# Five of nine pairs of groups of ph in seven half-products instead of eight, with sums of x and a list schedule in the source

## The chip, the cores and the metric

The kernel runs on one core of one Trainium2 chip. The metric is the device time of one execution in microseconds (us).

## What is computed

Attention with 2 x 12 heads of 448 rows and 64 columns, then two feed-forward stages on 896 rows of 768:

```
scores = 1/8 * q @ k.T, causal;  attn = softmax(scores) @ v
x = attn, heads side by side                              # 896 x 768
h = max(max(x @ w1, x @ w2), x @ w3)                      # 768 x 768 each
y = h @ w_out                                             # 768 x 768
out = elu(y @ w_in) @ w_out2                              # 768 x 2048, 2048 x 768
```

## The kernel before

Everything after attention is kept transposed: `x[b][k]` is tile k (128 of the 768 columns of x) of batch b, 128 x 2 x 448. Plane 0 holds the high part of the numbers (float32r) and plane 1 what is left of them. A weight tile is split in the same way into hi and lo. `products` (line 213) makes one product out of three matmuls per tile (a pass is one matmul of 448 columns): hi by plane 0 (L218), hi by plane 1 (L219), lo by plane 0 (L221).

ph is the product of x with w1, w2 and w3. For each of six column blocks f and each of the three weights n there is one *group*: six tiles, three passes, two batches, 36 passes, into two PSUM banks. `keep_best` (L230) copies the first product (ScalarE, L232) and takes the maximum with the others (VectorE, L234) into `best`. After n = 2, `best` is split into h (ScalarE L537, VectorE L146).

A weight arrives in 64-bit words that hold doubles. `load_w` (L185) issues its transfer on SP (L154) and turns it into hi and lo: three integer steps on VectorE (L199, L201, L202), a lift on ScalarE (L203), a combining step on VectorE (L204), hi on ScalarE (L208), lo on VectorE (L209). The first three weights (f = 0) are converted by another chain (`ahead_steps`, L157) during attention, and b = 0 of these groups is multiplied there, in TensorE's holes.

During attention `Plan` sets the order of work on all engines: each task has costs per engine, a due time (`LEADS`) and slots, and a list scheduler picks the next. After attention the source's own order and the framework set it: f = 0 for b = 1, then f = 1 to 5, then py (h by w_out), pg and po.

GpSimd has work in attention alone: it normalises the probabilities `pr` (L346).

Of the kernel before, what the change touches and what calls it, by code (L numbers as in the profile page):

```python
# [8 lines left out]
F32 = mybir.dt.float32  # L9
# [11 lines left out]
NPAIR = H // 2  # L21
# [17 lines left out]
SBANKS = 4  # L39

# [7 lines left out]
    "values3": -1.05, "warm": 2.09, "x_hi": 1.23, "x_lo": -1.04,  # L48
# [3 lines left out]
class Plan:  # L52
# [8 lines left out]
    LAG = {"PE": 210, "ACT": 150, "DVE": 125, "POOL": 90, "DMA": 2000}  # L61
# [8 lines left out]
    def add(self, fn, args, engines, pair, after=(), takes=(), gives=(), mode=None):  # L70
        lead = LEADS.get(f"{fn.__name__}{args[0]}" if args else None, LEADS.get(fn.__name__))
# [22 lines left out]
    def order(self):  # L94
        free = dict.fromkeys(self.LAG, 0)
# [28 lines left out]
def fused_kernel(ctx: ExitStack, tc: tile.TileContext, qk, v, w1, w2, w3, wo, wi2, wo2, outT):  # L124
# [32 lines left out]
    def ahead_steps(src, n, name, pool):  # L157
# [20 lines left out]
        hi, lo = (pool.tile([128, n, 128], F32R, tag=f"a_{m}", name=f"{m}_{name}") for m in ("hi", "lo"))  # L178
# [6 lines left out]
    def load_w(src, n, name):  # L185

# [39 lines left out]
    with ExitStack() as s1:  # L226
# [10 lines left out]
        ap_w = s1.enter_context(tc.tile_pool(name="ap_w", bufs=len(AHEAD)))  # L237
        ahead, bests, last = {}, {}, {}

        with ExitStack() as s2:  # L240
# [258 lines left out]
            kept = None  # L499
            for k in range(len(AHEAD)):  # L500
                block(k, weights(k))
            with tc.manual_schedule():
# [3 lines left out]
        hp = s1.enter_context(tc.tile_pool(name="hp", bufs=2 * NK))  # L506

        ctx.enter_context(tc.tile_pool(name="pad", bufs=1, side="right")).tile([128, 24], F32, name="pad")
        yp = ctx.enter_context(tc.tile_pool(name="yp", bufs=2 * NK, side="right"))
# [10 lines left out]
        h = [[None] * NK for _ in range(B)]  # L520
        for f in range(NK):
            best = [bests.get((f, b)) or bp.tile([128, S], F32, tag=f"best{b}", name=f"best{b}_{f}") for b in range(B)]
            for n, w in enumerate((w1, w2, w3)):
                over = range(1, B) if (f, n) in AHEAD else range(B)
                if (f, n) in AHEAD:
                    hi, lo = ahead[f, n]
# [99 lines left out]
```

## Time and profile before

| | |
|---|---|
| median of three runs | 505.23 us (504.86 to 505.77) |
| the profiled execution's own time | 505.17 us |
| its span, first to last instruction | 503.4 us |
| TensorE busy (matmul) | 497.0 us, 99% |
| VectorE busy | 313.9 us, 62% |
| ScalarE busy | 233.4 us, 46% |
| GpSimd busy | 41.0 us, 8% |
| granted TensorE clock | 1.00 |

A matmul of 448 columns is shown with 368 ns, but they are pipelined; what counts is how far apart they start. Durations on VectorE and ScalarE also overlap slightly with the next instruction's.

### The profile page before, as it was taken

The page shows a single profiled execution, that of the slowest core. Times are in us where ns is not written, and L with a number is a line of the kernel's source. Part 1 is how long each engine was busy: PE and PEld are TensorE (multiplying, and loading weights), DVE is VectorE, ACT ScalarE, POOL GpSimd, SP SyncE. Part 2 cuts the span into 40 slices and gives each one's busy share as a digit, 9 for nine tenths or more (in the row PEclk, how much of TensorE's full clock was granted, in tenths as well). Part 3 has the DMA queues.
Part 4 walks back from the last instruction along what each step waited for, and adds up shares of the span by engine and source line. Part 5 has one row for each costly group of instructions (what it writes and reads, how often), then busy time and mean ns, then how long its engine had stood idle before and what let it go on. Part 6 is the DMA issues. An engine that isn't in the chain of part 4 may idle for free.

```text
span 503.4 us, 6946 instructions
## 1 busy us (share of the span) xinstructions
PE 497.0 (99%) x2600; PEld 424.8 (84%) x2600; DVE 313.9 (62%) x664; ACT 233.4 (46%) x481; POOL 41.0 (8%) x96
## 2 busy tenths in 40 slices
PE   8999999999999999999999999999999999999997
PEld 3555757899999999999999999999999999999996
DVE  4999995477756656565656766776776544555310
ACT  5998794443333233332334665665664222222100
POOL 3475361000000000000000000000000000000000
PEclk9999999999999999999999999999999999999999
DMA  6626510055332331332332332332233434344000
GB/s 204 230 84 210 202 57 22 0 188 189 126 101 88 126 123 67 126 105 84 125 125 64 125 124 68 124 125 74 94 116 89 131 127 147 87 146 141 1 36 36
DMA packets 13969, 55.88 MB, mean 111 GB/s; under 512 B 1520, under 2 KB 3568, under 8 KB 13936
## 3 DMA queue, kind: packets, MB, share of 16 engines
q1 hardware_dynamic: 13936, 55.45, 32.9%
q8 instruction: 20, 0.33, 0.3%
q14 instruction: 13, 0.11, 0.1%
HBM read 52.69 MB, written 2.75 MB: 110 GB/s over the span
## 4 chain that ended last, share of the span: by engine, by line
PE 94%; DVE 2%; DMA 1%; POOL 1%; SPq 0%; ACT 0%; issue 0%; DVEq 0%; ACTq 0%
PE ph L218 9%; PE ph L221 9%; PE ph L219 9%; PE pg L221 8%; PE po L218 8%; PE po L219 8%; PE po L221 8%; PE pg L219 8%; PE pg L218 8%; PE pt L356 4%; PE o L379 4%; PE s L309 3%; PE py L221 3%; PE py L219 3%; PE py L218 3%; DVE pr L323 1%
## 5 line engine op out<-in xcount | busy, mean ns | idle before, releaser
L218 PE MATMUL ph<-x,hi_w 128*128 128x448 f32 x216 | 79.9, 370 | 0.0
L219 PE MATMUL ph<-x,hi_w 128*128 128x448 f32 x216 | 79.5, 368 | 0.0
L219 PE MATMUL po<-g,hi_wo 128*128 128x448 f32 x192 | 70.7, 368 | 0.0
L218 PE MATMUL po<-g,hi_wo 128*128 128x448 f32 x192 | 70.7, 368 | 0.0
L219 PE MATMUL pg<-y,hi_wi 128*128 128x448 f32 x192 | 70.5, 367 | 0.0
L218 PE MATMUL pg<-y,hi_wi 128*128 128x448 f32 x192 | 70.5, 367 | 0.0
L221 PE MATMUL ph<-x,lo_w 128*128 128x448 f32 x216 | 65.0, 368 | 0.0
L221 PE MATMUL po<-g,lo_wo 128*128 128x448 f32 x192 | 56.0, 368 | 0.0
L221 PE MATMUL pg<-y,lo_wi 128*128 128x448 f32 x192 | 55.1, 367 | 0.0
L203 ACT ACTIVATE f_wo<-f_wo,lift 128x768 uint32<-128x768 int16 (+1 forms) x24 | 21.2, 884 | 53.1 <-DVE f_wo L202 53.1
L208 ACT ACTIVATE hi_wo<-f_wo 128x768 fp32r<-128x768 f32 (+1 forms) x24 | 19.0, 792 | 56.1 <-PE po L219 38.8
L221 PEld LDWEIGHTS ph<-x,lo_w 128*128 128x128 f32 x216 | 40.5, 188 | 4.1
L209 DVE SCALAR_TENSOR_TENSOR lo_wo<-f_wo,hi_wo 128x768 fp32r<-128x768 f32 (+1 forms) x24 | 21.4, 891 | 36.3 <-ACT hi_wo L208 36.3
L218 PEld LDWEIGHTS ph<-x,hi_w 128*128 128x128 f32 x216 | 40.5, 188 | 4.0
L219 PEld LDWEIGHTS ph<-x,hi_w 128*128 128x128 f32 x216 | 40.6, 188 | 4.0
L218 PEld LDWEIGHTS po<-g,hi_wo 128*128 128x128 f32 x192 | 36.0, 188 | 3.7
L219 PEld LDWEIGHTS pg<-y,hi_wi 128*128 128x128 f32 x192 | 35.9, 187 | 3.8
L221 PEld LDWEIGHTS pg<-y,lo_wi 128*128 128x128 f32 x192 | 35.9, 187 | 3.8
L221 PEld LDWEIGHTS po<-g,lo_wo 128*128 128x128 f32 x192 | 36.0, 188 | 3.6
L219 PEld LDWEIGHTS po<-g,hi_wo 128*128 128x128 f32 x192 | 36.0, 188 | 3.6
L218 PEld LDWEIGHTS pg<-y,hi_wi 128*128 128x128 f32 x192 | 35.9, 187 | 3.7
L333 ACT ACTIVATE pr<-pr,nmx 128x384 f32<-128x384 f32 (+1 forms) x72 | 35.9, 501 | 5.8 <-DVE nmx L323 5.8
(88 smaller groups left out, 789.7 us busy)
## 6 DMA issues: line engine op xcount, KB each, us to landing
raw_w<-in_w SPq DMA_DIRECT2D x18, 768.0 KB, 4.5
raw_wi<-in_wi SPq DMA_DIRECT2D x16, 768.0 KB, 4.4
raw_wo<-in_wo SPq DMA_DIRECT2D x12, 768.0 KB, 4.3
raw_wo<-in_wo SPq DMA_DIRECT2D x12, 640.0 KB, 4.0
qk<-in_qk SPq DMA_DIRECT2D x11, 448.0 KB, 5.3
v<-in_v SPq DMA_DIRECT2D x12, 256.0 KB, 3.7
out_t<-ot SPq DMA_DIRECT2D x12, 224.0 KB, 3.0
qk<-in_qk SPq DMA_DIRECT2D x1, 256.0 KB, 3.4
```

The costliest lines, as they stand in the source:

```text
L203: nc.scalar.activation(f.bitcast(U32), y, AF.Relu, bias=lift, scale=2.0 ** 19)
L208: nc.scalar.mul(hi, fb, -1.0)
L209: nc.vector.scalar_tensor_tensor(out=lo, in0=fb, scalar=-1.0, in1=hi.bitcast(F32), op0=ALU.mult, op1=ALU.subtract)
L218: nc.tensor.matmul(ps, hi[:, c, :], xs[cc][:, 0, :], start=(cc == 0), stop=False)
L219: nc.tensor.matmul(ps, hi[:, c, :], xs[cc][:, 1, :], start=False, stop=False)
L221: nc.tensor.matmul(ps, lo[:, c, :], xs[cc][:, 0, :], start=False, stop=(cc == total - 1))
L309: nc.tensor.matmul(out, us[e]["qk"][own, 0, C * i:w], us[e]["qk"][own, 1, :w], start=True, stop=True, skip_group_check=True)
L323: nc.vector.tensor_tensor_reduce(out=pr, in0=u["s", g][j or 0][:, at:at + w], in1=mask_r if i == NB else mask[:, FULL - w:], scale=-0.125, ...
L333: nc.scalar.activation(pr, pr, AF.Exp, bias=u["nmx"][:, n:n + 1], scale=-1.0, accum_out=u["l"][:, n:n + 1])
L356: nc.tensor.transpose(pt[:e - C * c, at:at + C], u["pr", j if j is None else j ^ odd, i][:, C * c:e], ident)
L379: nc.tensor.matmul(u["o"][D * j:D * (j + 1), C * c:], u["v"][:, j, c], u["th_r"][:, j ^ odd] if c == NB else u["th"][:, c, j ^ odd, C * c: ...
```

## The change

With F1 and F2 two column blocks of one weight, u and d the upper and lower three tiles of the 768 rows, and x0, x1 the batches, the four outputs x0 F1, x0 F2, x1 F1, x1 F2 take eight half-products of 9 passes (three tiles, three passes). A *unit* takes seven, in Winograd's form of Strassen's algorithm. The sums of x are made once:

```
t0 = x1u + x1d     t1 = t0 - x0u     t2 = x0u - x1u     t3 = x0d - t1
```

and for each unit four differences of weights, "13": F2u - F1u and F2d - F2u, "24": F2d - 13u and F1d - 24u. The products, in TensorE's order (a, b, d, e are PSUM banks; `seed` copies the bank a to another, on which a later product adds):

```
a  = x0u F1u          b seeded from a
s5 = t0 13u           copied out of PSUM
a += t1 24u           d seeded from a
b += x0d F1d                               -> x0 F1
a += t2 13d           e seeded from a;  a + s5 -> x1 F2
d += t3 F2d                     d + s5         -> x0 F2
e += x1d 24d                               -> x1 F1
```

There are five units: blocks 1 and 2 for w2, w3; blocks 3 and 4 for w1, w2, w3. Blocks 0, 5 and w1 of 1 and 2 are left as groups. The new order is f = 0 (b = 1), f = 5, w1 of f = 1 and 2, then the units. The sums t (tiles t0_c to t3_c, c = 0 to 2, 24 operations; 19 are placed on GpSimd and 5 on VectorE) come from both planes of x; they are then split into planes (`whole`: 12 high halves on ScalarE, 12 low halves on VectorE). The stretch from f = 0 to the first two weights of py is list-scheduled by a second `Plan`. The order within attention stays, except that the transfers of the weights for f = 5 stand behind the last v transfers and that VectorE's first step on them lies at the end of attention.

```
+HALF = NK // 2
+UNITS = ((1, 2), (3, 4))
+FIRST = NK - 1
...
+            def add_totals(plan, c, engs, at, after, lead=None):
+                t1, t2, t3, t4 = (totals[q, c] for q in range(4))
...
+                for out, a, b, op in (
+                        (t4, h21, l21, ALU.add), (t1, t4, h22, ALU.add), (t1, t1, l22, ALU.add), (t2, h11, l11, ALU.add),
+                        (t3, t2, t4, ALU.subtract), (t2, t1, t2, ALU.subtract), (t4, h12, t2, ALU.subtract),
+                        (t4, t4, l12, ALU.add)):
...
+                        engines[eng].tensor_tensor(out=out, in0=a, in1=b, op=op)
...
+            add_totals(plan, 0, {"POOL": 950}, NPAIR + HALF, [xs_done[NPAIR + HALF]], 20)
+
+            begun = {k: load_steps((w1, w2, w3)[k][FIRST], NK, f"w{k}_{FIRST}") for k in range(2)}
...
+        late_plan = Plan({"raw": 0, "f": 2, "w": 0, "u": 7, "t": 4, "s5": 2, "m": 8, "best0": 1, "best1": 2})
+        PASS = 203.0
...
+        LOAD = (("DMA", 2000), ("DVE", 560), ("DVE", 356), ("DVE", 555), ("ACT", 937), ("DVE", 958))
+        LAST = (("ACT", 848), ("DVE", 958))
...
+        def leave(n, f, b, ps, after, gives, at, more=None):
+            if more is not None:
+                def both(eng):
+                    out = best_of(f, b) if n == 0 else ps[0]
+                    nc.vector.tensor_tensor(out=out, in0=ps[0], in1=more[0], op=ALU.add)
...
+        def whole(q, c):
+            def high(eng):
+                parts[q, c] = late.get((q, c)) or sp.tile([128, 2, S], F32R, tag="s", name=f"s{q}_{c}")
+                nc.scalar.copy(parts[q, c][:, 0], totals[q, c])
+            def low(eng):
+                sub(nc.vector, parts[q, c][:, 1], totals[q, c], parts[q, c][:, 0])
...
+        def unit(n, f1, f2):
...
+            t1 = less_of("13", up_, (1, up_), (0, up_), at, [opened, full[0], full[1]])
+            t3 = less_of("13", dn, (1, dn), (1, up_), at, [t1])
+            t2 = less_of("24", up_, (1, dn), ("13", up_), at, [t3])
+            t4 = less_of("24", dn, (0, dn), ("24", up_), at, [t2])
+            split(0, None, "w", at, [full[0]], slice(0, NK), [("u", name + "0", 2)])
+            split("13", "t", "t", at + 1800, [t3], slice(0, NK), [("u", name + "13", 2)])
+            split("24", "t", "t", at + 3600, [t4], slice(0, NK), [("u", name + "24", 1)])
+            split(1, None, "w", at + 9000, [full[1]], dn, [("u", name + "1", 2)])
...
+                    for c in range(HALF):
+                        w = xs[c] if sums is None else parts[sums, c]
+                        for m, (wt, i) in enumerate(((hi, 0), (hi, 1), (lo, 0))):
+                            nc.tensor.matmul(
+                                ps[0], wt[:, HALF * k + c], w[:, i, :], start=(new and c == m == 0),
+                                stop=(c == HALF - 1 and m == 2), skip_group_check=True)
...
+            t = product(a, 0, 0, a11, [], new=True)
+            sb = seed(a, b, t)
+            t5 = product(p, "13", 0, None, [], sums=0, new=True)
...
+            t = product(a, "24", 0, None, [sb], sums=1)
+            sd = seed(a, d, t)
+            t = product(b, 0, 1, a12, [sb], gives=["w"])
+            leave(n, f1, 0, b, [t], ["m"], clock[0] + 3000)
+            t = product(a, "13", 1, None, [sd], sums=2, gives=["t"])
+            se = seed(a, e, t)
+            leave(n, f2, 1, a, [t, t5, se], ["m", ("s5", name, 2)], clock[0] + 3000, s5)
+            t = product(d, 1, 1, None, [sd], sums=3, gives=["w"])
+            leave(n, f2, 0, d, [t, t5], ["m", ("s5", name, 2)], clock[0] + 3000, s5)
+            t = product(e, "24", 1, a22, [se], gives=["t"])
+            leave(n, f1, 1, e, [t], ["m"], clock[0] + 3000)
...
+        for f in sorted(set(range(NK)) - set(sum(UNITS, ()))):
+            for n in range(3):
+                standard(n, f, range(1, B) if (f, n) in AHEAD else range(B))
+        for f in UNITS[0]:
+            standard(0, f, range(B))
+        summed = [None] + [add_totals(late_plan, c, {"POOL": 950, "DVE": 619}, 0, [], 19000) for c in range(1, HALF)]
...
+        for fs_ in UNITS:
+            for n in range(1 if fs_ == UNITS[0] else 0, 3):
+                unit(n, *fs_)
+        wos = [load(wo[f], f"wo_{f}", clock[0] + 7300 * f)[0] for f in range(2)]
```

Three places of the order. The first is TensorE in w2 of blocks 1 and 2 before (ph{n}_{b}_{f}, two banks at a time):

```order
L218 MATMUL ph1_0_1_1481<-x1_481,hi_w1_1_1477 128x448
L219 MATMUL ph1_0_1_1481<-x1_481,hi_w1_1_1477 128x448
L218 MATMUL ph1_1_1_1482<-x7_1047,hi_w1_1_1477 128x448
L219 MATMUL ph1_1_1_1482<-x7_1047,hi_w1_1_1477 128x448
L221 MATMUL ph1_0_1_1481<-x1_481,lo_w1_1_1478 128x448
L221 MATMUL ph1_1_1_1482<-x7_1047,lo_w1_1_1478 128x448
```

and in a unit now, the second half of its second product (p13: s5, with t0, whose split planes are s0_c) and the start of the third (t1 as s1_c):

```order
L753 MATMUL p1302_1_1942<-s0_1_1485,hi13_2_1_1881 128x448 x2
L753 MATMUL p1302_1_1942<-s0_1_1485,lo13_2_1_1882 128x448
L753 MATMUL p1302_1_1942<-s0_2_1544,hi13_2_1_1881 128x448 x2
L753 MATMUL p1302_1_1942<-s0_2_1544,lo13_2_1_1882 128x448
L753 MATMUL p002_1_1928<-s1_0_1407,hi24_2_1_1886 128x448 x2
L753 MATMUL p002_1_1928<-s1_0_1407,lo24_2_1_1887 128x448
```

A bank gets its nine passes in a row, two with hi and one with lo for each tile.

The second place is VectorE after attention, where the next weights are converted beside f = 0, b = 1. Before:

```order
L204 SCALAR_TENSOR_TENSOR f_w0_1_1419<-raw_w0_1_1417,f_w0_1_1419 128x768
L204 SCALAR_TENSOR_TENSOR f_w1_1_1471<-raw_w1_1_1469,f_w1_1_1471 128x768
L209 SCALAR_TENSOR_TENSOR lo_w0_1_1426<-f_w0_1_1419,hi_w0_1_1425 128x768
L234 TENSOR_TENSOR best1_0_1348<-ph1_1_0_1369,best1_0_1348 128x448
L209 SCALAR_TENSOR_TENSOR lo_w1_1_1478<-f_w1_1_1471,hi_w1_1_1477 128x768
```

and now, with sums t among them (the sum into t1_1 reads what GpSimd made):

```order
L542 TENSOR_TENSOR t3_2_104<-x8_1166 128x448
L212 SCALAR_TENSOR_TENSOR f_w0_5_1402<-raw_w0_5_1180,f_w0_5_1402 128x768
L212 SCALAR_TENSOR_TENSOR f_w1_5_1414<-raw_w1_5_1237,f_w1_5_1414 128x768
L542 TENSOR_TENSOR t1_1_97<-t0_1_94,t1_1_97 128x448
L260 TENSOR_TENSOR best1_0_1437<-ph1_1_0_1417,best1_0_1437 128x448
L218 SCALAR_TENSOR_TENSOR lo_w0_5_1449<-f_w0_5_1402,hi_w0_5_1448 128x768
```

The first low half has moved behind one sum and one maximum.

The third place is VectorE within a unit now (f0 and f1 are the two weights, f13 and f24 the differences); before, a weight took the steps L199 to L209 alone:

```order
L208 TENSOR_TENSOR f1_2_1_1825<-f1_2_1_1825 128x768
L212 SCALAR_TENSOR_TENSOR f0_2_1_1809<-raw_w2_1_1743,f0_2_1_1809 128x768
L212 SCALAR_TENSOR_TENSOR f1_2_1_1825<-raw_w2_2_1794,f1_2_1_1825 128x768
L724 TENSOR_TENSOR f13_2_1_1863<-f1_2_1_1825,f0_2_1_1809 128x384
L724 TENSOR_TENSOR f13_2_1_1863<-f1_2_1_1825 128x384
L724 TENSOR_TENSOR f24_2_1_1879<-f1_2_1_1825,f13_2_1_1863 128x384
L724 TENSOR_TENSOR f24_2_1_1879<-f0_2_1_1809,f24_2_1_1879 128x384
L218 SCALAR_TENSOR_TENSOR lo0_2_1_1858<-f0_2_1_1809,hi0_2_1_1857 128x768
L260 TENSOR_TENSOR best0_1_1784<-ps01_1_1842,best0_1_1784 128x448
L218 SCALAR_TENSOR_TENSOR lo13_2_1_1882<-f13_2_1_1863,hi13_2_1_1881 128x768
```

Both weights' integer steps stand ahead of the first combining step; the differences follow, and the low halves of three weight tiles share the queue with the outputs.

## Rows read from the trace of the kernel before

**Rows 1.** The page's chain that ended last, share of the span by engine

```profile
PE 94%; DVE 2%; DMA 1%; POOL 1%; SPq 0%; ACT 0%; issue 0%; DVEq 0%; ACTq 0%
```

**Rows 2.** Windows, f = 2 to 5: stretch, length, each engine's busy time, clock, DMA share

```profile
142.60:217.00 74.40, 74.40 (x361) 67.57 (x361) 44.36 (x70) 23.68 (x33) 0.00 (x0) 1.00 0.30 105
```

**Rows 3.** Timeline of TensorE: start, duration, line, operation, tiles, forms, count

```profile
94.19 0.47 PE L218 MATMUL ph<-x,hi_w 128*128 128x448 f32 x1
...
105.44 0.37 PE L218 MATMUL ph<-x,hi_w 128*128 128x448 f32 x1
...
106.27 0.57 PE L221 MATMUL ph<-x,lo_w 128*128 128x448 f32 x2
...
217.04 0.37 PE L218 MATMUL py<-h,hi_wo 128*128 128x448 f32 x1
```

**Rows 4.** Timeline of VectorE, 99 to 104 us, idle time before in brackets

```profile
99.64 1.83 DVE L204 SCALAR_TENSOR_TENSOR f_w<-raw_w,f_w 128x768 int32<-128x768 int32 x2 [1.20 <-ACT f_w L203]
101.51 0.96 DVE L209 SCALAR_TENSOR_TENSOR lo_w<-f_w,hi_w 128x768 fp32r<-128x768 f32 x1
102.39 0.62 DVE L234 TENSOR_TENSOR best<-ph,best 128x448 f32<-128x448 f32 x1
102.92 0.95 DVE L209 SCALAR_TENSOR_TENSOR lo_w<-f_w,hi_w 128x768 fp32r<-128x768 f32 x1
```

**Rows 5.** Timeline at attention's end; the v and raw_w transfers (durations in ns; landing)

```profile
79.31 0.40 POOL L346 TENSOR_SCALAR pr<-pr,r 128x128 f32<-128x128 f32 x1
...
84.13 0.53 ACT L252 CAST x<-o 128x448 fp32r<-128x448 f32 x1 [0.50 <-PE o L379]
...
L295 SPq DMA_DIRECT2D v<-in_v x5: 328/328/1776, 47.1 to 75.0; - x5
...
DMA to landing us min/median/max: 4.2/4.5/6.7
...
80.34 0.45 DVE L346 TENSOR_SCALAR pr_None<-pr_None,r 128x448 f32<-128x448 f32 x1
...
82.34 0.62 DVE L234 TENSOR_TENSOR best<-ph,best 128x448 f32<-128x448 f32 x1 [1.55 <-PE ph L221]
...
83.92 0.92 PE L379 MATMUL o<-th,v 128*64 128x448 f32 x4
```

**Rows 6.** GpSimd's line 346: duration ns min/median/max, first and last start, forms

```profile
L346 POOL TENSOR_SCALAR pr<-pr,r x57: 365/480/1231, 10.6 to 79.3; 128x384 f32<-128x384 f32 x19, 128x256 f32<-128x256 f32 x19, 128x128 f32<-128x128 f32 x19
...
L346 POOL TENSOR_SCALAR pr_None<-pr_None,r x5: 632/646/993, 17.7 to 78.7; 128x448 f32<-128x448 f32 x5
```

**Rows 7.** Groups by form (count, busy us, mean ns, idle before); last row: waits

```profile
L199 DVE TENSOR_SCALAR f_w<-raw_w 128x768 bf16<-128x768 bf16 x15 | 8.3, 559 | 3.9 <-DMA raw_w<-in_w 3.7
...
L201 DVE TENSOR_SCALAR f_w<-f_w 128x768 int16<-128x768 int16 x15 | 5.3, 358 | 0.3
...
L202 DVE TENSOR_TENSOR f_w<-f_w 128x768 int16<-128x768 int16 x15 | 8.3, 557 | 0.4
...
L204 DVE SCALAR_TENSOR_TENSOR f_w<-raw_w,f_w 128x768 int32<-128x768 int32 x15 | 14.3, 957 | 11.9 <-ACT f_w L203 11.9
...
L234 DVE TENSOR_TENSOR best<-ph,best 128x448 f32<-128x448 f32 x24 | 14.0, 620 | 21.7 <-PE ph L221 21.7
...
L146 DVE TENSOR_TENSOR lo_w<-f_w,hi_w 128x768 fp32r<-128x768 f32 x3 | 2.9, 954 | 0.6 <-ACT hi_w L180 0.6
...
L203 ACT ACTIVATE f_w<-f_w,lift 128x768 uint32<-128x768 int16 x15 | 14.0, 937 | 28.2 <-DVE f_w L202 28.1
...
L232 ACT COPY best<-ph 128x448 f32<-128x448 f32 x12 | 5.8, 527 | 3.6 <-issue 2.9 <-PE ph L221 0.7
...
DVE f_w L204 <- ACT f_w L203: 11.9, 11, 1.2
```

**Rows 8.** Timeline of GpSimd and VectorE at 29 us

```profile
29.04 1.06 POOL L346 TENSOR_SCALAR pr<-pr,r 128x128 f32<-128x128 f32 x1
...
28.75 1.11 DVE L172 SCALAR_TENSOR_TENSOR f_w<-raw_w,f_w 128x768 int32<-128x768 int32 x1
```

More of the change, by code (lines that the diff above doesn't have):

```diff
@@ L92, in begins, with order @@
         return min((at + t["engines"][e], at, e) for e, at in ready.items())
[L94 to L95 removed]
+    def order(self, free=()):
+        free = dict.fromkeys(self.LAG, 0) | dict(free)
         left, out = list(self.tasks), []
@@ L518, in psum @@
             return pool.tile([128, S], F32, tag=tag, name=name)
-        h = [[None] * NK for _ in range(B)]
-        for f in range(NK):
[L522 to L526, printed above, removed]
-                else:
-                    with tc.issue_after(last["DVE"].ins):
-                        hi, lo = load_w(w[f], NK, f"w{n}_{f}")
-                ps = [psum(f"ph{n}_{b}_{f}") for b in over]
-                products(ps, hi, lo, [x[b] for b in over], 0, NK, NK)
-                for b in over:
-                    keep_best(best[b], ps[b - over[0]], n)
-            for b in range(B):
-                hs = hp.tile([128, 2, S], F32R, tag="h", name=f"h{b}_{f}")
-                nc.scalar.copy(hs[:, 0], best[b])
-                sub(nc.vector, hs[:, 1], best[b], hs[:, 0])
-                h[b][f] = hs
@@ new lines, in fused_kernel, with convert, step @@
+        LOAD = (("DMA", 2000), ("DVE", 560), ("DVE", 356), ("DVE", 555), ("ACT", 937), ("DVE", 958))
+        LAST = (("ACT", 848), ("DVE", 958))
+        def convert(steps, costs, at, took, gave, begun=False):
+            got, t = [], None
+            def step(eng):
+                got[:] = [next(steps)]
+            for k, (eng, cost) in list(enumerate(costs))[begun:]:
+                t = task(step, eng, cost, at, [t], takes=took.get(k, ()), gives=gave.get(k, ()))
+            return got, t
@@ new lines, in finish, with standard, product @@
+        def finish(f, b, at, after):
+            def high(eng):
+                nc.scalar.copy(h[b][f][:, 0], best_of(f, b))
+            def low(eng):
+                sub(nc.vector, h[b][f][:, 1], best_of(f, b), h[b][f][:, 0])
+            t = task(high, "ACT", 570, at, [after])
+            hs_done[f, b] = task(low, "DVE", 617, at, [t], gives=[f"best{b}"])
+        def standard(n, f, over):
+            at, ps = clock[0], {b: [] for b in over}
+            parts, t = (([ahead[f, n]], None) if (f, n) in AHEAD else load(
+                (w1, w2, w3)[n][f], f"w{n}_{f}", at, begun.pop(n, None) if f == FIRST else None))
+            def product(eng):
+                for b in over:
+                    ps[b].append(psum(f"ph{n}_{b}_{f}"))
+                products([ps[b][0] for b in over], *parts[0], [x[b] for b in over], 0, NK, NK)
+            t = on_pe(product, 18 * len(over), [t], takes=["m"] * len(over), gives=["w"])
+            for b in over:
+                leave(n, f, b, ps[b], [t], ["m"], clock[0] + 2000)
```

176 lines of the change are left out of this document (156 added, 20 removed).

## The prediction

> **What bounds the kernel now.** I read the chain of waits first, then windows, then the timeline. The chain is TensorE for 94% of the span [rows 1]. TensorE's granted clock is 1.00 in the stretch that the change rewrites, and TensorE is busy for all of its 74.40 us, with VectorE busy for 44.36 (60%) and ScalarE for 23.68 (32%) [rows 2]. The timeline gives the rate. From 105.44 to 217.04 us stand the 15 groups f = 1 to 5, 540 passes of 448 columns: 111.60 / 540 = 0.2067 us each, without a gap [rows 3]. The three groups f=0, b=1 before them write one PSUM bank at a time: 54 passes from 94.19 to 105.44, 0.208. So a pass costs the same whether two banks alternate or one is used. In this stretch a pass less is 0.2067 us less, as long as weights and inputs come in time; nothing else is on the path.
>
> **Removed.** A pair of groups takes 2 x 36 = 72 passes; a unit takes seven half-products of 9, so 63. Five units save 45 passes: 45 x 0.2067 = **-9.30 us**. The same rate holds in a unit, because its passes are f=0's pattern (two with the high part, one with the low, into one bank) with the same shapes.
>
> **Added, on the path only if late.**
>
> *Weights for the first new group, f=5.* Its first matmul with the low half stands four passes after its start at 105.44, at 106.27 [rows 3]. A matmul that was late would need its weights loaded first, for which I allow 0.25 us: the limit is 106.0. Before, the same place in VectorE's queue made the low half from 101.51 to 102.46, behind two combining steps from 99.64 [rows 4]. Now a sum (0.53) and the maximum of ph (0.53; before, it stood behind) come ahead: 103.5. Start to start I take a row's duration less 0.09, as 102.39 and 102.92 show for 0.62 [rows 4]. Margin 2.5 us: **0**. f=1's low half is due at 128.2 (another 108 passes, 22.3 us, later). Up to it VectorE's new order has 19 steps of 0.53 (12 low halves of sums and three more sums among them), 10.1; two and a half conversions of 2.34, 6.1; three low halves of weights, 2.6. That is 18.8 of 24.7 us, with 6 spare for its waits: **0**.
>
> *GpSimd's sums.* There are 19 now, the first behind the last normalisation, at 79.31 + 0.40 = 79.7, the rest behind x9's high part, done at 84.13 + 0.53 = 84.66 [rows 5]. No row has a two-input operation on GpSimd. Its one-input one takes 632 ns for 448 columns and 365 for 128 at the fastest [rows 6], 0.83 ns a column; with every column read twice I estimate 632 + 0.83 x 448 = 1.00 us, bounded by 0.63 (the second input is free) and 1.7 (below). VectorE's sum t1_1 waits for GpSimd's t2_1, the twelfth behind x9: 84.7 + 12 x 1.00 = 96.7, before VectorE is there at 101.4 (the combining steps end at 99.64 + 1.83). **0**; the bound of 1.7 is a rival.
>
> *The weight transfers for f=5* now stand behind four v transfers on SP's queue, the last of which was issued at 75.0 [rows 5]. Landing takes 4.2 to 6.7 us [rows 5], so 79.7 to 81.7. VectorE meets its first step on them ahead of a short reciprocal (0.2), the normalisation of 80.34 and a maximum. Before, it idled there 1.55 us until 82.34 [rows 5]. At the latest landing, 0.56 + 0.20 + 0.45 end at 82.95 and the maximum at 83.6; the PSUM bank that it frees is taken at 83.92 [rows 5]. **0**.
>
> *VectorE in the units.* Durations are from [rows 7]; a step that waits for VectorE's own last result begins 0.04 after it ends, any other 0.09 before. The differences of weights are 384 columns wide; between 448 (0.620) and 768 (0.954) a column costs 1.04 ns, so 0.55 each. Conversion for one unit: two weights at 0.60 + 0.40 + 0.47 + 0.87, four differences together 2.2, low halves 3 x 0.87 + 0.47: 4.7 + 2.2 + 3.1 = 10.0 us. Outputs: two additions of the fifth product and four maxima, 3.4 us (1.1 where n = 0). Both together are 13.4, against 63 x 0.2067 = 13.0 us of TensorE: on its own, a unit is slightly more than VectorE can do. While TensorE runs the five units (65.1 us), VectorE owes four conversions (the first was due earlier) 40, outputs 4 x 3.4 + 1.1 - 0.5 (the last comes after) = 14.2, low halves of h for f=1, 2: 2.1, and two weights of wo less one low half 5.5. That makes 61.8, or **95%**, with 3.3 us spare for all its waits. In the stretch before, it waited for ScalarE's lift 1.1 us a time (11.9 us in 11) [rows 7]. The new order runs two weights' integer steps ahead of both combining steps, so 1.5 us of the second cover the 0.94 of the first lift, and the second lift is late by about 0.15; ScalarE is busy with other work at times. Bounds: 0 (waits fit into the spare), and 5 x 1.1 - 3.3 = 2.2 (one uncovered wait in each unit). I take **+1.0**, nearer to the covered case.
>
> *Seeds.* Three times in a unit ScalarE copies a PSUM bank to another, and a product later TensorE adds onto the copy. No row has a copy into PSUM; the nearest, out of PSUM, is 0.53 [rows 7]. One product covers 9 x 0.2067 = 1.86 us: room for a lift of 0.94, just begun, and the copy of 0.53. With two such long steps ahead (1.88 + 0.53, and 0.25 for the weights) it would be 0.8 late. Bounds 0 and, once a unit, 5 x 0.8 = 4.0; I take **0**, as ScalarE has about 7.1 us of work in a unit of 13.0.
>
> **Sum**: 505.17 (the profiled execution's own time, 0.06 below the median of the runs) - 9.30 + 1.0 = **496.9 us**. The likeliest case runs from 495.6 (no wait, run noise) to 498.0.
>
> **A port of the chip, weighed.** At 29.04 GpSimd's 128-column operation took 1.06 us where 365 ns is its fastest; VectorE was 0.29 us into a 768-column step with two SBUF inputs that took 1.11 where 0.96 is usual [rows 6 to 8]. So the one that came second lost 0.7 and the other 0.15. By the Trainium skill (SBUF — State Buffer, section Who interferes with whom), a VectorE instruction with two SBUF inputs and a GpSimd instruction that reads SBUF share a port that one holds for its whole duration, while the other waits; by that rule GpSimd's sums and VectorE's low halves would exclude each other. The trace agrees in the row at 29.04. By the rule the time would be the one that rival 2 works out from rows; by the estimate of 1.00 us alone it is the sum above.
>
> **Rivals.**
>
> 1. *VectorE becomes the bound.* For it: 95% of its time is owed. Against: its order is interleaved so that it seldom waits. With one uncovered wait a unit (2.2) the time is 498.1; with two (11.0 - 3.3 = 7.7), 503.6. Chance 0.18.
>
> 2. *GpSimd's sums are held up as at 29.04*: every sum 1.00 + 0.7 = 1.7 us. Then VectorE's t1_1 is free at 84.7 + 12 x 1.7 = 105.1, f=5's low half 2.0 later at 107.1, 1.1 late. GpSimd has five more sums behind t1_1 before VectorE's last two sums can go, and from there to f=1's low half it is 14.9 us of work (of the 18.8) and some 1.5 of waits: 105.7 + 8.5 + 0.6 + 16.4 = 131.2, due at 128.2 + 1.1: another 1.9. Together 3.0: 505.17 - 9.30 + 1.0 + 3.0 = 499.9. Against: most of the twelve run while attention ends, up to 94.19 [rows 3], when VectorE mostly drains PSUM. Chance 0.08.
>
> 3. *GpSimd's sum is dear in itself, and the kernel gets slower.* The first stall starts at 86.8 + 12p = 106.0, p = 1.6 us. At p = 2.0 the two stalls are 4.8 and 3.3 and eat the gain of 8.3: that is the point. At 2.2 (six times 365 ns) they are 7.2 and 4.2: 496.9 + 11.4 = 508.3. For it: no row prices this operation. Against: it is twice the estimate. Chance 0.05.
>
> That the passes are not saved is excluded by the order: it has 603 for ph's 648. What is left, 0.04, is a loss about as large as the gain that I have not seen.
>
> **How the numbers follow.** Likeliest 0.65, rivals 0.18, 0.08 and 0.05, no difference 0.04. About 0.2% (1.0 us) is what a measurement of this kernel can tell: faster 0.65 + 0.18 + 0.08 = 0.91, same 0.04, slower 0.05. The range reaches from 495.6 to 500.2: it takes in rival 2 and the better part of rival 1, and leaves out some 0.17.
>
> **What would show it.** Right: 603 matmuls of 448 columns in place of ph's 648 (288 under the old lines, 315 on the units' own), 0.2067 us apart, and py starts about 8 us earlier, near 208.8; VectorE is over 90% busy in the units; GpSimd's sums take about 1.0 us and end before 110; TensorE's few idle stretches stand at the first low half of a late unit and are put down to VectorE. Wrong: idle time at f=5's or f=1's first matmuls, released by VectorE behind GpSimd (rivals 2 and 3); gaps of over half a microsecond in every unit (rival 1, or ScalarE's seeds); passes farther apart in a unit.

## The result, and the profile after

| | before | changed |
|---|---|---|
| median of five runs | 505.60 us (504.86 to 506.09) | 490.36 us (489.36 to 495.23) |
| the profiled execution's own time | 505.17 us | 489.36 us |
| its span | 503.4 us | 487.6 us |
| TensorE / VectorE / ScalarE / GpSimd busy | 497.0 / 313.9 / 233.4 / 41.0 | 480.1 / 351.6 / 254.0 / 65.5 |

The ratio is 0.9714 [0.9663, 0.9764]. The change saves 15.2 us of medians, 15.8 of the profiled executions; I had forecast 8.3, and 490.36 lies below the range. Four of the five runs lie between 489.4 and 490.8 and one, of which there is no trace, at 495.2.

The chain is still TensorE's (page, part 4; [rows 1] before):

```profile
PE 90%; DVE 6%; DMA 1%; POOL 1%; ACT 1%; issue 0%; SPq 0%; DVEq 0%; ACTq 0%
```

The surprise stands in stages that the change does not touch. Here are the matmuls of py, pg and po on TensorE (duration in ns, then first and last start), before:

```profile
L218 PE MATMUL py<-h,hi_wo x72: 368/368/368, 217.0 to 260.9; 128*128 128x448 f32 x72
...
L218 PE MATMUL pg<-y,hi_wi x192: 363/367/368, 261.7 to 379.9; 128*128 128x448 f32 x192
...
L218 PE MATMUL po<-g,hi_wo x192: 363/368/368, 380.7 to 499.1; 128*128 128x448 f32 x192
```

and changed:

```profile
L244 PE MATMUL py<-h,hi_wo x72: 362/365/369, 208.2 to 251.2; 128*128 128x448 f32 x72
...
L244 PE MATMUL pg<-y,hi_wi x192: 362/362/367, 252.0 to 366.4; 128*128 128x448 f32 x192
...
L244 PE MATMUL po<-g,hi_wo x192: 362/365/370, 367.2 to 483.3; 128*128 128x448 f32 x192
```

From start to start, py's 216 passes took 44.7 us and now 43.8; pg's 576 took 119.0 and now 115.2. So the spacing, the time from one pass's start to the next one's, was 0.2067 before and is 0.2027 (py, po) and 0.2000 (pg) now, with the same code and the same granted clock:

```profile
209.00:251.00 42.00, 42.00 (x209) 38.91 (x209) 32.10 (x52) 17.68 (x26) 0.00 (x0) 1.00 0.39 136
253.00:366.00 113.00, 113.00 (x567) 106.04 (x566) 82.66 (x142) 71.35 (x123) 0.00 (x0) 1.00 0.32 106
```

These are windows, with [rows 2]'s columns: the clock is 1.00, TensorE never idle. (A matmul that reaches into a window is counted, so a window holds nearly two more than fit.)

Where does the spacing change? The timeline of TensorE, changed kernel, at f=5's start:

```profile
105.92 0.37 PE L244 MATMUL ph<-x,hi_w 128*128 128x448 f32 x1
106.13 0.37 PE L245 MATMUL ph<-x,hi_w 128*128 128x448 f32 x1
107.03 0.68 PE L247 MATMUL ph<-x,lo_w 128*128 128x448 f32 x2 [0.53 <-DVE lo_w L218]
```

Up to 106.13 the starts are 0.2067 apart. The first matmul with the low half starts 0.69 later than that spacing, because VectorE made the low half late; from there to 128.8 the starts are 0.2027 apart. At 129.18, f=1's low half, there is a second wait, of 0.15 beyond the spacing, and behind it 0.2067 again, to 147.19, the next wait. Behind that one 0.2027 stays through three more waits to py's end. Then, with no wait, 0.2000 for all of pg and 0.2027 for po.

Added up from the starts of TensorE's matmuls behind attention, against 0.2067 each:

| term | us |
|---|---|
| 45 passes fewer x 0.2067 | -9.30 |
| spacing: ph's groups -0.44, units -1.17, py -0.87, pg -3.84, po -2.30 | -8.61 |
| waits beyond the spacing, 2.10 for 0.10 before | +2.00 |
| start of f=0, b=1 (94.25 for 94.19) | +0.07 |
| sum (the spans differ by 15.8) | -15.84 |

Without the second term the time would be 497.9, inside the range. So the question is what shortens all the passes.

Why the low half came late is in the trace as well. Timeline of VectorE, changed kernel:

```profile
94.93 0.62 DVE L150 TENSOR_TENSOR x<-o,x 128x448 fp32r<-128x448 f32 x1 [2.48 <-ACT x L280]
95.47 1.56 DVE L150 TENSOR_TENSOR h<-best,h 128x448 fp32r<-128x448 f32 x1
96.95 1.31 DVE L206 TENSOR_SCALAR f_w<-f_w 128x768 int16<-128x768 int16 x1
98.30 1.39 DVE L208 TENSOR_TENSOR f_w<-f_w 128x768 int16<-128x768 int16 x1
...
100.20 0.36 DVE L206 TENSOR_SCALAR f_w<-f_w 128x768 int16<-128x768 int16 x1
100.59 0.56 DVE L208 TENSOR_TENSOR f_w<-f_w 128x768 int16<-128x768 int16 x1
...
101.61 2.78 DVE L212 SCALAR_TENSOR_TENSOR f_w<-raw_w,f_w 128x768 int32<-128x768 int32 x2
...
105.38 3.42 DVE L218 SCALAR_TENSOR_TENSOR lo_w<-f_w,hi_w 128x768 fp32r<-128x768 f32 x2
```

and of GpSimd:

```profile
93.08 3.47 POOL L542 TENSOR_TENSOR t<-t,x 128x448 f32<-128x448 f32 x3
96.51 1.55 POOL L542 TENSOR_TENSOR t<-x 128x448 f32<-128x448 f32 x1
98.13 1.15 POOL L542 TENSOR_TENSOR t<-t,t 128x448 f32<-128x448 f32 x1
101.83 1.74 POOL L542 TENSOR_TENSOR t<-t,x 128x448 f32<-128x448 f32 x1 [2.55 <-DVE t L542]
```

The three steps of VectorE from 95.47 on, beside GpSimd's sums, took 4.26 us; the same steps take 0.62, 0.36 and 0.56 where GpSimd idles (the run e10_sums_vectore below; the last two also at 100.20). The step at 94.93, which reads one of its inputs from PSUM, took 0.62 although GpSimd was busy. The 2.7 us of difference are the margin of 2.5 and more, and they are not all: the two combining steps from 101.61 took 2.78 for 1.83 before [rows 4], and the first of the two low halves from 105.38 took 1.59 for 0.95.

### The profile page after: what moved, and what is told of

Read it like the earlier page. It is cut to its first block, busy times and chain, and to the rows that moved or that the text cites. A ratio compares the mean times of both kernels' runs of the same rounds, so it can differ in the third digit from the quotient of the medians.

```text
span 487.6 us, 6964 instructions
## 1 busy us (share of the span) xinstructions
PE 480.1 (98%) x2555; PEld 416.4 (85%) x2555; DVE 351.6 (72%) x721; ACT 254.0 (52%) x521; POOL 65.5 (13%) x115
## 3 DMA queue, kind: packets, MB, share of 16 engines
HBM read 52.69 MB, written 2.75 MB: 114 GB/s over the span
## 4 chain that ended last, share of the span: by engine, by line
PE 90%; DVE 6%; DMA 1%; POOL 1%; ACT 1%; issue 0%; SPq 0%; DVEq 0%; ACTq 0%
PE po L245 8%; PE po L244 8%; PE po L247 8%; PE pg L245 8%; PE pg L247 8%; PE pg L244 8%; PE p L753 7%; PE ps L753 5%; PE pt L384 4%; PE o L407 4%; PE s L337 3%; PE ph L247 3%; PE ph L244 3%; PE ph L245 3%; PE py L245 3%; PE py L244 3%
## 5 line engine op out<-in xcount | busy, mean ns | idle before, releaser
L245 PE MATMUL pg<-y,hi_wi 128*128 128x448 f32 x192 | 69.6, 363 | 0.0
L244 PE MATMUL pg<-y,hi_wi 128*128 128x448 f32 x192 | 69.6, 362 | 0.0
L247 PE MATMUL pg<-y,lo_wi 128*128 128x448 f32 x192 | 54.0, 362 | 0.0
L244 PE MATMUL ph<-x,hi_w 128*128 128x448 f32 x96 | 35.7, 371 | 0.0
L245 PE MATMUL ph<-x,hi_w 128*128 128x448 f32 x96 | 35.2, 367 | 0.0
L212 DVE SCALAR_TENSOR_TENSOR f_wo<-raw_wo,f_wo 128x768 int32<-128x768 int32 (+1 forms) x24 | 21.3, 891 | 18.9 <-ACT f_wo L210 18.9
L374 POOL TENSOR_SCALAR pr<-pr,r 128x384 f32<-128x384 f32 (+2 forms) x57 | 30.2, 548 | 12.3 <-DVE r L370 6.8
L351 DVE CUSTOM_DVE_ANT_0 pr<-s,mask 128x384 f32<-128x384 f32 (+1 forms) x72 | 26.6, 412 | 7.0 <-PE s L337 6.9
L247 PE MATMUL ph<-x,lo_w 128*128 128x448 f32 x96 | 30.6, 369 | 0.5 <-DVE lo_w L218 0.5
```

Source lines behind the costliest of these rows:

```text
L212: nc.vector.scalar_tensor_tensor(out=f, in0=below, scalar=13, in1=f, op0=ALU.logical_shift_right, op1=ALU.bitwise_or)
L244: nc.tensor.matmul(ps, hi[:, c, :], xs[cc][:, 0, :], start=(cc == 0), stop=False)
L245: nc.tensor.matmul(ps, hi[:, c, :], xs[cc][:, 1, :], start=False, stop=False)
L247: nc.tensor.matmul(ps, lo[:, c, :], xs[cc][:, 0, :], start=False, stop=(cc == total - 1))
L351: nc.vector.tensor_tensor_reduce(out=pr, in0=u["s", g][j or 0][:, at:at + w], in1=mask_r if i == NB else mask[:, FULL - w:], scale=-0.125, ...
L374: engines[eng].tensor_scalar(out=u["pr", j, i], in0=u["pr", j, i], scalar1=u["r"][:, n:n + 1], scalar2=1.0, op0=ALU.mult, op1=ALU.mult)
```

## The experiments

**Theory.** TensorE's passes can run at more than one steady spacing with the same instructions. A wait of TensorE draws the spacing anew (after it either one can come), and it then lasts. In the long one every pass takes 0.2067; in the short one its time depends on the distance between the addresses of the moving tile and the weights. Before, TensorE was in the long one when attention ended and nothing made it wait again.

**Rivals.** (a) The units, the sums or the new order make passes shorter. (b) The address alone decides. The compiled programs give the addresses in a partition: x, h, g and the sums lie 0 or 256 bytes from the weights modulo 512, y 160 or 416, as the kernel's unused tile `pad` shifts it; so modulo 256 (the two planes agree in that) the distance is 0, for y 160. It is the same before and after. (c) It is the length of the wait, or the fall of the granted clock behind a long one, that makes the passes shorter.

**A wait alone.**

```diff
+                if (f, n) == (1, 0):
+                    for _ in range(12):
+                        nc.gpsimd.tensor_scalar(
+                            out=lo[:, 0], in0=lo[:, 0].bitcast(F32), scalar1=1.0, scalar2=1.0, op0=ALU.mult, op1=ALU.mult)
                 ps = [psum(f"ph{n}_{b}_{f}") for b in over]
```

> The kernel before with nothing changed but the moment at which f=1's first low half of weights is ready: twelve multiplications by one on GpSimd (0.37 to 0.4 us each by attention's row) stand behind VectorE's low half, so that it comes some 0.5 to 2 us after TensorE wants it (106.3). Theory (the spacing of passes has more than one steady value, and a wait of TensorE at such a place can change it): behind the wait the passes lie 0.2027 us apart in ph, py and po and 0.2000 in pg, as in the changed kernel; 1,330 passes x 0.0040 + 576 x 0.0067 = 9.2 us less, the wait of about 1 us more: 497, faster without one pass removed. Rival (the shorter spacing belongs to the units, the sums or where the new tiles lie): 0.2067 everywhere, 506 to 507.

Measured: 501.01 us (ratio 0.9907 [0.989, 0.9924]). The wait was 3 us, longer than meant, and the granted clock fell behind it (timeline, then windows):

```profile
105.38 0.37 PE L219 MATMUL ph<-x,hi_w 128*128 128x448 f32 x1
108.49 0.68 PE L221 MATMUL ph<-x,lo_w 128*128 128x448 f32 x2 [2.75 <-POOL lo_w L533]
```

```profile
110.00:114.00 4.00, 4.00 (x13) 3.58 (x13) 2.30 (x4) 1.06 (x2) 0.00 (x0) 0.58 0.85 233
114.00:200.00 86.00, 86.00 (x426) 79.69 (x426) 52.63 (x85) 29.23 (x40) 0.00 (x0) 1.00 0.34 118
```

Both together cost 4.5 us beyond the spacing. From 113.6 to the end the passes are 0.2027 apart, in pg 0.2000: 9.1 us less. One wait, made by twelve multiplications on GpSimd, does what no row of the kernel before had shown. It does not always do it: one of the four runs took 508.02 us, by its time the wait with the long spacing behind it. That run's mean granted clock was 1.000, that of the other three 0.996 to 0.997, so this kernel alone does not exclude rival (c). With eight multiplications for twelve:

> The run e1_stall with eight multiplications for twelve: in that run they took 0.547 us each and ended at 108.44, 3.1 us late, behind which the granted clock was 0.58 for 4 us; eight end at 106.3, 0.7 late. Theory (any wait draws the spacing anew; a short one leaves the clock alone): 505.2 - 9.2 + 0.7 = 496.7 where the short spacing is drawn, 506 where not. Rival (the shorter spacing came from the long wait or from the clock's fall): 0.2067 throughout, 506 in all.

Measured: the four runs gave 496.36, 496.59, 505.0 and 505.36 (a median of 500.79 that none of them has); the profiled one is the first:

```profile
105.78 0.37 PE L219 MATMUL ph<-x,hi_w 128*128 128x448 f32 x1
106.47 0.67 PE L221 MATMUL ph<-x,lo_w 128*128 128x448 f32 x2 [0.33 <-POOL lo_w L533]
106.98 0.36 PE L218 MATMUL ph<-x,hi_w 128*128 128x448 f32 x1
```

A wait of 0.5 us beyond the spacing, the clock stays at 1.00, and behind it 0.2027 and 0.2000. So the fall of the clock is not needed, and rival (c)'s second half falls. The theory's two values are both there. For the two runs at 505 there is no trace; that they drew the long spacing is read from their times.

**The groups in the changed kernel's order.** The units and the split of the sums into planes are left out, the sums stay.

```diff
-        for f in sorted(set(range(NK)) - set(sum(UNITS, ()))):
+        for f in (0, 5, 1, 2, 3, 4):
...
-        for fs_ in UNITS:
-            for n in range(1 if fs_ == UNITS[0] else 0, 3):
-                unit(n, *fs_)
```

> The changed kernel without its units: all blocks as groups of 36 passes (648 instead of 603), no splitting of the sums, but with its list schedule, its order (f=5 behind f=0) and the sums of x themselves, so that f=5's first low half is late as in the changed kernel. Theory (waits set the spacing): a wait at 106 and 0.2027 behind it, in pg 0.2000: about 490.4 + 45 x 0.2027 = 499.5, so that some 6 us of the gain need no pass removed. Rival (the units make the shorter spacing): 0.2067 throughout, 505 to 506.

Measured: 497.96 us (0.9852 [0.9838, 0.9867]), with all 648 passes: two waits at f=5, 0.2027 behind them, 0.2000 in pg. Without the sums too:

```diff
-            add_totals(plan, 0, {"POOL": 950}, NPAIR + HALF, [xs_done[NPAIR + HALF]], 20)
...
-        summed = [None] + [add_totals(late_plan, c, {"POOL": 950, "DVE": 619}, 0, [], 19000) for c in range(1, HALF)]
```

> The groups in the list schedule, as in the run e4_groups_listed (497.96), and without the 24 sums of x as well; the output needs none of them there. Theory (GpSimd's sums slow VectorE's steps down at 95 to 100 us, that makes f=5's first low half 0.9 us late, and that wait puts TensorE into the shorter spacing): without the sums VectorE's three steps take 0.62, 0.36 and 0.56 again for 1.56, 1.31 and 1.39, the low half is in time, no wait, 0.2067 throughout: 505, slower by 7 us than with the 24 operations. Rival (the order of the list schedule or f=5 behind f=0 makes the shorter spacing): 497 to 498.

Measured: 505.14 us in ten runs (504.33 to 505.77; 0.9993 [0.9981, 1.0005]). Nothing waits behind attention, and all 1,962 passes are 0.2067 apart. To take 24 operations out costs 7.2 us, because they had made TensorE wait. Windows of the first and the second kernel:

```profile
148.00:180.00 32.00, 32.00 (x159) 29.66 (x158) 21.27 (x35) 11.13 (x15) 0.00 (x0) 1.00 0.35 119
...
265.00:365.00 100.00, 100.00 (x502) 93.84 (x501) 72.95 (x124) 65.00 (x112) 0.00 (x0) 1.00 0.33 108
```

```profile
148.00:180.00 32.00, 32.00 (x156) 29.07 (x155) 18.74 (x30) 10.82 (x16) 0.00 (x0) 1.00 0.31 102
...
265.00:365.00 100.00, 100.00 (x486) 90.48 (x485) 70.54 (x119) 61.67 (x105) 0.00 (x0) 1.00 0.29 100
```

The same stretch of pg holds 502 passes or 486. Rival (a) falls: the first kernel has no units, the two share the code and, but for the sums, the order.

**Many waits.** The kernel before; the loads of py, pg and po but the last one get, with `hold` from two to four:

```diff
+            for _ in range(hold if c == 1 else 0):
+                one = lo[:, 0:2, 0:1]
+                nc.gpsimd.tensor_scalar(
+                    out=one, in0=one.bitcast(F32), scalar1=1.0, scalar2=1.0, op0=ALU.mult, op1=ALU.mult)
```

> The kernel before with a short wait of TensorE put into each of the 39 loads of weights in py, pg and po but the last: two, three or four multiplications by one on GpSimd (0.2 to 0.25 us each) between the first and the second low pass of a group, which touch two columns of the low half and so can neither begin before the one nor end after the other; waits of 0.1 to 0.8 us. Theory (a wait draws the spacing anew, by the moment at which it ends): both spacings appear, 0.2067 and 0.2027 (0.2000 in pg), each constant from one wait to the next, the short one the more often. Rival (the spacing changes once, for good, or by what VectorE and GpSimd do): one spacing from the first wait to the end. The time itself, 510 to 525, tells nothing.

Measured, in one execution (523.32 us): behind 8 of the 39 waits the passes were 0.2067 apart (1 of 6 in py, 3 of 16 in pg, 4 of 17 in po), behind the other 31 0.2027, in pg 0.2000, each time constant up to the next wait. Two stretches of pg, 33 spacings each, one with 6.60 us, the next with 6.82 (297.53 - 290.71):

```profile
283.00 0.36 PE L222 MATMUL pg<-y,hi_wi 128*128 128x448 f32 x1
...
289.60 0.36 PE L223 MATMUL pg<-y,hi_wi 128*128 128x448 f32 x1
290.20 0.67 PE L225 MATMUL pg<-y,lo_wi 128*128 128x448 f32 x2 [0.24 <-POOL lo_wi L219]
290.71 0.37 PE L222 MATMUL pg<-y,hi_wi 128*128 128x448 f32 x1
...
297.53 0.36 PE L223 MATMUL pg<-y,hi_wi 128*128 128x448 f32 x1
```

The length of the wait does not decide, and with that the rest of rival (c) falls: from the last matmul before it to the first one behind it are 0.596 us at 290.20, which drew the long spacing, and 0.595 at 338.25, which drew the short one. What decides is left open.

**The addresses.** A tile that nothing uses, ahead of the weights (the kernel before, then the changed one):

```diff
+    ctx.enter_context(tc.tile_pool(name="shift", bufs=1)).tile([128, 8], F32, name="shift")
     wp = ctx.enter_context(tc.tile_pool(name="wp", bufs=2))
```

> The kernel before with an unused 32-byte tile ahead of the weight pool, so that weights, x, h and g begin on multiples of 64 bytes, as y alone does now (compiled addresses: y 0, all others 32 past a multiple of 64). Theory (the kernel before is in the slow spacing, in which y's passes take 0.2067 like all others, so the address decides nothing there): 0.2067 everywhere, 505.2. Rival (the address alone decides the spacing): 0.2000 from x on, 1,960 passes x 0.0067 less: 492.

Measured: 498.83 us (0.9871 [0.9843, 0.99]); neither had it. The short spacing was there from attention's holes on (0.2027 at 79 us), with no wait behind 94 us; ph, py and po at 0.2027. But y is now at distance 128, and pg took 0.2040. So the spacing is drawn in attention's holes too: in the run e5_no_sums the hole at 79 us has 0.2025 and that at 85 us 0.2067. Addresses bear on that draw. In all seven traces of kernels with an unused tile added in these experiments the passes right behind attention (94 us) are in the short spacing, in all seven without one in the long spacing, and all 32 runs of the kernel before took between 504.58 and 507.05. Why is not shown. The four runs here were 497.42 and 497.61, 500.04 and 500.37; the first alone has a trace, and what adds 2.6 to 2.8 us to the last two is open.

> The changed kernel with the same unused 32-byte tile. Theory (in the fast spacing the address of the tiles decides between 0.2027 and 0.2000): where the changed kernel's passes lay 0.2027 apart they lie 0.2000 apart: about 500 passes of ph, 216 of py and 576 of po x 0.0027 = 3.4 us less, 486 to 487, if the waits still put it into the fast spacing. Rival (0.2000 in pg has another cause than y's address): 490, py and po at 0.2027.

Measured: 492.1 us (0.9743 [0.9727, 0.9759]), no faster than the changed kernel. Both expectations failed: all operands on multiples of 64 did not give 0.2000; the units ran at 0.2027, py at 0.2067 from a wait at 197 on, pg at 0.2040, po at 0.2027 (windows in py, pg and po):

```profile
220.00:248.00 28.00, 28.00 (x138) 25.43 (x137) 19.47 (x31) 11.40 (x17) 0.00 (x0) 1.00 0.43 143
265.00:365.00 100.00, 100.00 (x492) 92.08 (x491) 71.78 (x122) 63.89 (x110) 0.00 (x0) 1.00 0.33 106
385.00:478.00 93.00, 93.00 (x460) 86.18 (x460) 40.59 (x66) 22.53 (x30) 0.00 (x0) 1.00 0.32 101
```

This corrects the theory. From 197 us on TensorE did not wait, and yet py has the long spacing and pg and po a short one: the long spacing ended where pg began, at 252.3, where the distance goes from 0 to 128. So a wait is not the only thing that can end a spacing. In the kernel before, the step from py to pg (0 to 160) did not end it. Nor is it the multiple that counts. y's own distance was the next thing to try, with the unused tile behind the weights:

```diff
     wp = ctx.enter_context(tc.tile_pool(name="wp", bufs=2))
+    ctx.enter_context(tc.tile_pool(name="shift", bufs=1)).tile([128, 104], F32, name="shift")
```

> The kernel before with an unused tile of 416 bytes behind the weight pool, so that x, h and g begin 96 bytes ahead of a multiple of 512 from the weights, as y alone does now. Theory (in the short spacing the distance between the addresses of the two operands decides: 0.2000 at y's distance, 0.2027 at 0 and 256): if TensorE falls into the short spacing in a hole of attention as in the run e2_before_64, 0.2000 in all stages, 505.25 - 1,960 x 0.0067 = 492; if it does not, 0.2067 and 505. Rival (0.2000 belongs to pg's own work, not to the distance): ph, py and po keep 0.2027 at best, 497 or more.

Measured: **492.33 us** (0.9741 [0.9716, 0.9767]). f=0 still has distance 0 to its weights and 0.2027; from f=1 to the end all passes are 0.2000 apart:

```profile
148.00:180.00 32.00, 32.00 (x162) 30.03 (x161) 20.68 (x34) 11.90 (x17) 0.00 (x0) 1.00 0.34 120
220.00:248.00 28.00, 28.00 (x142) 26.28 (x141) 17.22 (x28) 10.55 (x16) 0.00 (x0) 1.00 0.32 113
265.00:365.00 100.00, 100.00 (x502) 93.84 (x501) 73.58 (x126) 64.56 (x112) 0.00 (x0) 1.00 0.31 106
385.00:478.00 93.00, 93.00 (x467) 87.28 (x466) 41.80 (x67) 22.96 (x31) 0.00 (x0) 1.00 0.33 107
```

416 unused bytes give 12.8 us, without a pass removed. The same in the changed kernel:

> The changed kernel with the same unused tile. Theory: passes of ph, py and po in the short spacing go from 0.2027 to 0.2000, except those of the units with the differences of weights (their tiles move with x, distance 0): py 216, po 576 and some 300 of ph x 0.0027 = 2.9 us less, 487 to 488; more if no wait throws it back to 0.2067 as at 129 to 146 us of the changed kernel (0.3). Rival (distance decides nothing): 490.

Measured: 487.28 us (0.9638 [0.9617, 0.966]). Then the tiles of the weights' differences too:

```diff
             for tag, bufs in (("u", 7), ("t", 4), ("s5", 2)):
+                if tag == "t":
+                    up.enter_context(tc.tile_pool(name="shift_t", bufs=1)).tile([128, 24], F32, name="shift_t")
```

> The run e7_after_off96 (487.28) with an unused tile of 96 bytes ahead of the tiles that hold the differences of weights, so that every pass of the units too has its operands at y's distance. In the run before, the units' passes lay 0.2029 apart on average (308 passes). Theory (distance decides in the short spacing): 0.2000, 0.9 us less: 486.4. Rival (the units have something of their own, seeds or one bank at a time, that lengthens them): 487.3.

Measured: 487.0 us (0.9637 [0.9614, 0.966]), its profiled run 485.74. The units' passes lie 0.2000 apart, where they lay 0.2029; the medians don't tell the two kernels apart. One run in four of each lay at 496, 9 and 10 us above the traced one. No trace shows why; the long spacing from the wait at 197 on (1,419 passes, nearly all 0.0067 longer) would add 9.4 and 9.5. The changed kernel's run at 495.2 is 5.8 above the traced one, where the long spacing from its wait at 197 on would add 7.2; its cause stays open. Both beat the kernel before and, by their medians, the changed one.

Four more distances at once, in the kernel before:

```diff
+    ctx.enter_context(tc.tile_pool(name="shift_x", bufs=1)).tile([128, 8], F32, name="shift_x")
...
+        s1.enter_context(tc.tile_pool(name="shift_h", bufs=1)).tile([128, 8], F32, name="shift_h")
...
-        ctx.enter_context(tc.tile_pool(name="pad", bufs=1, side="right")).tile([128, 24], F32, name="pad")
+        ctx.enter_context(tc.tile_pool(name="pad", bufs=1, side="right")).tile([128, 40], F32, name="pad")
...
+    ctx.enter_context(tc.tile_pool(name="shift_g", bufs=1)).tile([128, 40], F32, name="shift_g")
```

> The kernel before with unused tiles that put the moving tile at other distances from the weights in each stage (modulo 256 bytes, by which the two planes agree): x 32, h 64, y 96, g 192, where 0 gave 0.2027, 128 gave 0.2040 and 160 gave 0.2000. Theory (distance decides): each stage has a constant value of its own between 0.2000 and 0.2067, unless the long spacing is drawn, 0.2067 in all. Rival (a stage has its value by its own work): py and po 0.2027, pg 0.2000 or 0.2040, as in the other runs.

Measured, in one execution (499.75 us): x at 32 gave 0.2067, h at 64 0.2000, y at 96 0.2053, g at 192 0.2022, each constant, with no wait between them; f=0, b=1 before them, at distance 0, had 0.2027. The values at 64, 96 and 192 are the short spacing's. That at 32 can be read in two ways: either the short spacing has no gain there, or TensorE fell into the long one where the distance changed, as it left it in the run e3_after_64. Each stage's windows, in that order:

```profile
148.00:180.00 32.00, 32.00 (x156) 29.11 (x155) 18.86 (x31) 11.19 (x16) 0.00 (x0) 1.00 0.31 102
220.00:248.00 28.00, 28.00 (x141) 26.25 (x141) 17.09 (x28) 10.55 (x16) 0.00 (x0) 1.00 0.33 113
265.00:365.00 100.00, 100.00 (x489) 91.40 (x488) 71.25 (x120) 62.84 (x109) 0.00 (x0) 1.00 0.32 104
385.00:478.00 93.00, 93.00 (x462) 86.20 (x461) 44.92 (x72) 24.91 (x33) 0.00 (x0) 1.00 0.37 116
```

Rival (b) falls with the two spacings at one distance (pg before and after); as half of the cause it stands.

**Sums on VectorE.** The kernel of the run e9_after_all96 and

```diff
-        summed = [None] + [add_totals(late_plan, c, {"POOL": 950, "DVE": 619}, 0, [], 19000) for c in range(1, HALF)]
+        summed = [None] + [add_totals(late_plan, c, {"DVE": 619}, 0, [], 19000) for c in range(1, HALF)]
```

> The run e9_after_all96 with the 16 sums of c = 1, 2 that remain after attention's own order on VectorE alone (5 of them were there; 11 more at 0.53 us are 5.9 us more for VectorE). Theory (GpSimd's sums cost VectorE more by holding its steps up than they take off it): the wait at f=5 (1.1 us beyond its spacing) goes, that at f=1 (0.5) goes or shrinks: 485 or less. Rival (VectorE's time is what is short, 95% busy): f=1's and the units' waits grow by as much or more: 487 to 490.

Measured: 489.87 us (0.9704 [0.9688, 0.972]), slower. The theory's first half holds: with GpSimd idle VectorE's three steps are short, and f=5 waits for nothing (timeline of VectorE):

```profile
95.79 0.62 DVE L151 TENSOR_TENSOR h<-best,h 128x448 fp32r<-128x448 f32 x1
96.32 0.35 DVE L207 TENSOR_SCALAR f_w<-f_w 128x768 int16<-128x768 int16 x1
96.71 0.56 DVE L209 TENSOR_TENSOR f_w<-f_w 128x768 int16<-128x768 int16 x1
```

The rival's half decides: at 130.00 TensorE stood still for 2.50 us in front of a group of f=1, for weights that VectorE had not got to.

```profile
130.00 0.47 PE L245 MATMUL ph<-x,hi_w 128*128 128x448 f32 x1 [2.50 <-ACT hi_w L231]
```

All waits together were 6.1 us for 3.3 in the run e9_after_all96.

## Why the prediction was wrong, point by point

**The rate (failed, and it decided).** The prediction said: "In this stretch a pass less is 0.2067 us less, as long as weights and inputs come in time; nothing else is on the path." The 45 passes did save 9.30. What failed is the rest of the sum: 505.17 - 9.30 + 1.0 has no term for the 1,917 passes that stay, so it puts a change of their price at nothing, without a reason. That price is no constant; the term measured -8.6. All of before's passes behind attention lay 0.2067 apart, so its trace showed one value only. But in the run e1_stall, where the granted clock was 0.51 (110.5 to 113.4 us), the passes lay 0.373 apart, which is 448 columns at the lower level, 1.2 GHz; from that row I estimate 0.187 at the upper level, 2.4 GHz, and I never asked what the other 0.020 was. The run e1_stall, with a wait alone, has the same effect: 9.1 us of spacing.

**The margin at f=5 (failed, 0.7 us).** "Margin 2.5 us: 0." It was late by 0.69, and f=1's low half, with "6 spare", by 0.15. I had looked for the late GpSimd sum that VectorE needs, and priced VectorE's own steps as if alone. That is rival 2's port, with the victim exchanged: I let GpSimd's sums pay 0.7 each, and VectorE's first three steps paid 0.94, 0.95 and 0.83, the combining steps 0.95, the first low half 0.64. The run e10_sums_vectore, in which GpSimd idles there, shows it. By the Trainium skill (SBUF — State Buffer, section Who interferes with whom) the one that issued first keeps the port for its whole instruction and the other waits; the rows agree: each of these steps of VectorE was late by less than the 1.15 of a sum. Rival 2's waits were 1.1 and 1.9, priced as loss, at a chance of 0.08. Both came, smaller, and with the first the short spacing began, which gave back more than the waits took. That the change came out better than forecast is luck: the extra gain hangs on a wait that I had counted as a loss. Together with the units' 1.0 the waits measured +2.0, where the sum has +1.0.

**GpSimd's sum.** Estimated 1.00, bounded by 0.63 and 1.7: 1.13 to 1.18 where VectorE left it alone, up to 1.87 beside it. The last one ended at 113.5, not before 110. Rival 3's price (2.0) did not occur.

**VectorE in the units (right).** VectorE was busy for 59.00 of the 62 us from 145 to 207, 95% as worked out, and the units' waits beyond the spacing add up to 1.0, the +1.0 that I took:

```profile
145.00:207.00 62.00, 61.85 (x303) 56.22 (x302) 59.00 (x100) 35.90 (x56) 0.00 (x0) 1.00 0.34 115
```

**Seeds, transfers.** I took 0 for each. In the run e7_after_off96 one wait of 0.5 us is put down to ScalarE's copy; in the changed kernel none is. The transfers of f=5's weights delayed nothing: f=0, b=1 began 0.06 later.

**py near 208.8.** It was 208.2, but for two reasons that nearly cancel: 1.6 us of spacing saved in ph and 1.0 of waits more than forecast.

What the change itself is worth is seen where both kernels have all passes behind f=0 at 0.2000: 492.26 (the profiled run of e6_before_off96) and 485.74 (that of e9_after_all96), one execution each, 6.5 us: 9.0 for the passes less 3.2 of waits, and 0.7 before f=0, b=1.

## What to carry to other kernels

Before pricing a removed matmul by its spacing, compare the spacing with columns over clock, and look whether a few bytes between the moving tile and the weights, or one short wait (it did so in two runs of four), change it for every pass; here 416 unused bytes gave 12.8 us and a rewriting of the product 6.5 on top. When an expected gain comes out too large, look at the stages that were not touched. And where work moves to GpSimd, charge VectorE's steps beside it, not only GpSimd's.

## What the runs showed of the hardware that I had not expected

- The same matmuls (448 columns, float32r, weights changed for each) ran at a constant 0.2067 or at a shorter constant spacing, at a granted clock of 1.00 in both. A wait of TensorE could change which (behind 8 of 39 it was the long one), and it lasted until the next wait, over 1,400 passes in the changed kernel. Once it changed without a wait, from long to short, where the distance between the operands changed (e3_after_64, 252.3 us). What decides a draw is open.
- The short spacing by the distance of the moving tile from the weights, modulo 256 bytes: 0: 0.2027; 32: 0.2067 (or the long spacing); 64: 0.2000; 96: 0.2053; 128: 0.2040; 160: 0.2000; 192: 0.2022 (32, 64, 96 and 192 from one execution). Why, and whether it is the modulus or the full distance that counts, no run here shows. By the Trainium skill (TensorE: Matmul & The Clock Gate, section Step-by-step: what each phase is for) weights and moving tile come through independent read ports, so that loading the one takes nothing from the other; by that the distance would not matter. The runs differ, and they decide.
- In the run e1_stall TensorE stood idle for 2.75 us, and the granted clock then fell (0.58 from 110 to 114 us, passes up to 0.373 apart). In the run e10_sums_vectore it stood idle for 2.50 us, and the clock stayed at 1.00 (130 to 138 us).
- VectorE's 16-bit steps of 768 columns (0.36 and 0.56) took 1.31 and 1.39 beside GpSimd's two-input additions, which took 1.15 alone and up to 1.87 beside VectorE.
